# Hash attention and two MLPs on one core: the second head's first hashes one pass later, and the first weights of the next layer converted in consecutive passes

## The chip, the core and the metric

One core of a Trainium2 chip runs the whole program in one launch. The metric is device time in microseconds (us); lower is better. TensorE (PE in the rows) multiplies, VectorE (DVE) and ScalarE (ACT) work element by element, GpSimd (POOL) does some element work on the side, and SyncE (SP) issues the transfers, one after the other in its own order. Each engine works through its own list of instructions in order and waits for the others by semaphores.

## What is computed

Attention in which a query sees only the keys of its own hash bucket, then two MLPs on the result:

```
q_bits = (q @ proj > 0);  k_bits = (k @ proj > 0)          # 6 bits each
mask   = bucket(q_bits) == bucket(k_bits)
attn   = softmax(where(mask, q @ k.T / sqrt(64), -1e9))     # 2 x 8 heads, 768 x 768
x      = attn @ v                                           # 1536 tokens x 512
x      = (silu(x @ w_gate) * (x @ w_val)) @ w_out           # 512 -> 1536 -> 512
h      = x @ w_in;  out = (layernorm(h * softmax(h)) * g_ln) @ w_out2
```

The MLP weights arrive as 64-bit floats. The kernel reads them as pairs of 32-bit words and makes 32-bit floats of them on VectorE.

## The kernel before

**Attention in passes.** The 16 heads are 8 pairs. One pass of the main loop (line 754 and following; its counter is i) takes 128 queries of one head against all 768 keys, so a pair has 12 passes and there are 96. The work is a pipeline over passes. In pass i the loop issues, in this order: `maxima(i)` and `biases(i)` on VectorE (L495, L504); on TensorE `transposes(i - 2)`, which turn the exponentials of pass i - 2 into a two-buffer PSUM tile (L535); hashing and turning work of a later pair; `scores(i + 1)` into a two-buffer PSUM tile (L484); for pass i - 2 the rounding on ScalarE (`highs`, L544) and the rest on VectorE (`lows`, L548), which read the turned exponentials; `values` for an earlier quarter (L570, L574); and `exps(i)` on ScalarE (L520), which read the scores. So the transposes of pass i wait for the `lows` issued in pass i - 1, which free their PSUM buffer, and `scores(i + 1)` wait for `exps(i - 1)`.

**Hashes.** `hashes(p, n)` multiplies the turned heads with the hash weights and VectorE turns signs to bits (L448); four transfers (`move`, L264) then carry the bits of both heads to their places. For the first pair each head has its own `first_hashes(j)`: eight matrix products (L355) into the PSUM tiles `pp` and `av`, which have one buffer each, and then the bits. For the second head (j = 1) the generator is started at line 773; its second step, the bits (L364) and two moves, follows in pass 2.

**First weights.** `early()` (line 713) prepares the first block of `w_gate` and of `w_val`. For each it issues a transfer of 512 KB into one buffer `raw` (L717) and then six VectorE instructions (`to_float32`: L47, L51, L53, L57, L62, L64, in this order). It is a generator: every `go(first_weights)` does one step, and a step is either the transfer or one instruction. The `w_gate` transfer is issued ahead of the loop. So the steps in the loop are six instructions, the `w_val` transfer, and six instructions. Since there is one buffer, the second transfer waits for the last instruction on the first block. The results `w1f` are first used behind the attention (L844).

**What sets the order.** The order on every engine is that in which the code is written (`manual_schedule`). SP's list too: a transfer is issued only when all transfers written ahead of it have been issued, each after its own wait.

Of the kernel before, what the change touches and what calls it, by code (L numbers as in the profile page):

```python
# [28 lines left out]
def run(steps):  # L29
    for _ in steps:  # L30
        pass
# [36 lines left out]
def hash_attention_then_two_mlps(  # L68
# [137 lines left out]
    with at:  # L206
# [13 lines left out]
        SLOTS = 2 * C  # L220
# [3 lines left out]
        def load(p, nm):  # L224

            if p >= len(pairs):
                return
            b, hp = pairs[p]
            t = nat.tile([P, 2, C, D], F32, tag=nm, name=nm)
            src = {"q": q, "k": k, "v": v}[nm]  # L230
            nc.sync.dma_start(
                t, src[b, 2 * hp:2 * hp + 2].rearrange("h (p c) d -> p h c d", c=C)
            )
            raw[p, nm] = t
# [230 lines left out]
        def quarter(h):  # L465


            p, l = divmod(h, 4)
            return (p, l // 2, l % 2) if p == 0 else (p, l % 2, l // 2)
# [5 lines left out]
        def scores(i):  # L475
            if not 0 <= i < NSLOT:
                return
            p, j, n = quarter(i // CH)
            x, c = turned[p, j], n * CH + i % CH
            s = ps_s.tile([P, 2, 512], F32, tag="s", name="s")  # L480
            rows = slice(c * P, (c + 1) * P)
            for a, m, first in ((x["qa"], x["ka"], True), (x["qb"][:MB], x["kb"][:MB], False)):
                for n in range(2):
                    nc.tensor.matmul(  # L484
                        s[:, n, :HALF], a[:, rows], m[:, n * HALF:(n + 1) * HALF],
                        start=first, stop=not first,
                    )
            s_of[i] = s

        def maxima(i):  # L490
            if not 0 <= i < NSLOT:
                return

            top = tops[i % len(tops)]
            nc.vector.tensor_reduce(  # L495
                top[:, 1:2], s_of[i][:, :, :HALF], AX.XY, ALU.max, negate=True
            )

        def biases(i):
            if not 0 <= i < NSLOT:  # L500
                return
            top = tops[i % len(tops)]
            nm = sm.tile([P, 2], F32, tag="nm", name="nm", bufs=3)
            biased = nc.vector.scalar_tensor_tensor(  # L504
                nm, top[:, 1:2].to_broadcast([P, 2]), LONE, top, ALU.is_lt, ALU.mult
            )
            if i > 2:
                bias_of[:] = [biased]
            nm_of[i] = nm
# [16 lines left out]
        def transposes(i, g):  # L526
            if not 0 <= i < NSLOT:
                return
            h, c = divmod(i, CH)
            if c == 0 and g == 0:  # L530
                eh_of[h] = et.tile([P, C, HALF], R32, tag="eh", name="eh")
                el_of[h] = et.tile([P, C, HALF], R32, tag="el", name="el")
            t = ps_t.tile([P, CH, P], F32, tag="t", name="t")
            for m in range(CH):
                nc.tensor.transpose(t[:, m, :], e_of[i][:, g, m * P:(m + 1) * P], idf)  # L535
            t_of[i, g] = t
# [5 lines left out]
        def highs(i, g):  # L542
            if 0 <= i < NSLOT:
                nc.scalar.copy(half_tile(eh_of, i, g), t_of[i, g])  # L544

        def lows(i, g):
            if 0 <= i < NSLOT:
                last_of[i] = nc.vector.tensor_sub(  # L548
                    half_tile(el_of, i, g), t_of.pop((i, g)),
                    half_tile(eh_of, i, g).bitcast(F32),  # L550
                )
# [108 lines left out]
        def go(work):  # L660

            next(work, None)
# [3 lines left out]
        def turning(p, l):  # L666

            if p == 1:

                at = {  # L670
                    0: lambda: turn(p + 1, 0, 2),
                    1: lambda: turn(p + 1, 1, 0),
                    2: lambda: turn(p + 1, 1, 1),
                    3: lambda: turn(p + 1, 1, 2),
                    6: lambda: hashes(p + 1, 0, False),
                    7: lambda: hashes(p + 1, 1, False),
                }
            else:
                if l in (4, 6):
                    hashing[:] = [hashes(p + 1, l // 6)]  # L680
                at = {
                    0: lambda: turn(p + 1, 1, 0),
                    1: lambda: turn(p + 1, 1, 1),
                    3: lambda: turn(p + 1, 1, 2),
                }
                at.update({n: lambda: hashing[0] for n in range(4, 8)})
            at.update({
                9: lambda: turn(p + 2, 0, 0),
                10: lambda: turn(p + 2, 0, 1),
                11: lambda: turn(p + 2, 0, 2),  # L690
            })
            return at[l]() if l in at else iter(())

        def beginning(i):

            at = {
                3: lambda: (turn(1, 0, 0), turn(1, 0, 1, 1)),
                4: lambda: (turn(1, 0, 2), turn(1, 1, 0, 1)),
                5: lambda: (turn(1, 1, 1),),
                6: lambda: (turn(1, 1, 2),),  # L700
                8: lambda: (hashes(1, 0, False),),
                9: lambda: (hashes(1, 1, False),),
                10: lambda: (turn(2, 0, 0),),
                11: lambda: (turn(2, 0, 1),),
            }
            works = at[i]() if i in at else ()
            for work in works:
                go(work)
            yield
            for work in works:  # L710
                go(work)

        def early():

            for n, w in enumerate((w_gate, w_val)):
                t = wp.tile([P, DM], I64, name="raw")
                nc.sync.dma_start(  # L717
                    t.rearrange("p (k f) -> p k f", k=KD),
                    w[:, 0:P].rearrange("(k p) f -> p k f", p=P),
                )  # L720
                yield
                yield from to_float32(nc, t, w1f[n])
                yield
# [22 lines left out]
        with tc.manual_schedule():  # L746
            for p, nm in ((1, "k"), (1, "q"), (0, "v")):
                load(p, nm)
            first_weights = early()
            go(first_weights)  # L750
            hashed = start()
            done = leaving = iter(())
            splits = {}
            for i in range(NSLOT + 9):
                p, l = divmod(i, SLOTS)
                h, part = divmod(i - 5, CH)
                if i < SLOTS:
                    work = beginning(i)
                else:
                    work = turning(p, l)  # L760
                if part == 0:
                    leaving, done = done, results(h - 1)
                    go(done)
                maxima(i)
                if part == 0 and h - 1 >= NQ - 2:
                    go(done)
                biases(i)
                transposes(i - 2, 0)
                if i == 0:
                    go(hashed)  # L770
                transposes(i - 2, 1)
                go(work)
                if i == 1:
                    hashed = first_hashes(1)
                    go(hashed)
                scores(i + 1)
                for g in range(2):
                    highs(i - 2, g)
                    lows(i - 2, g)
                if part == 0:  # L780
                    go(leaving)
                values(h, part)
                if part == 2 and h == NQ - 1:
                    spread(*quarter(h)[::2])
                go(work)
                if i == 2:
                    go(hashed)
                exps(i)
                if i == 0:
                    for of, nm in ((1, "k"), (1, "q"), (0, "v")):  # L790
                        run(split(of, nm))
                splitting(p, l)
                go(done if part == 2 else leaving)
                if part == 2 and h == NQ - 2:
                    widen(*quarter(NQ - 1)[::2], "both")
                if part == 1:
                    go(done)
                    sums(h + 1)
                if l in (3, 9, 11):
                    go(first_weights)  # L800

    AHEAD = 2
# [374 lines left out]
```

## Time and profile before

| | |
|---|---|
| three runs | 699.26, 701.16, 701.88 us; median 701.16 |
| the profiled execution: its time | 700.81 us |
| the profiled execution: its span | 699.0 us |
| busy share of the span | PE 99%, VectorE 80%, ScalarE 49%, GpSimd 21% |
| granted TensorE clock, mean | 0.993 of full speed |

The span runs from the first to the last instruction; the execution's own time is 1.81 us longer. The attention takes about the first 250 us of it; the two MLPs follow. The shares are means over stages. Times in the rows count from the start of the span.

### The profile page before, as it was taken

To read this page: it belongs to the slowest core of one execution; us is meant where nothing else is said; L and a number is where in the kernel's file an instruction comes from. 1 tells how busy PE (TensorE), PEld (TensorE's weight loads), DVE (VectorE), ACT (ScalarE), POOL (GpSimd) and SP (SyncE) were. 2 spreads that over 40 slices of the span, in tenths; PEclk is the share of its full clock that TensorE was granted. 3 is DMA by queue.
4 is the path that set the end of the run, shared out by engine and by line. 5 is a ranking of instruction groups with operands and counts; after the bars stand their busy time and mean duration, and the time that the engine had idled before them with its cause. 6 is when DMAs were issued, how large, how long until landed. Compare 5 with 4: busy or idle time off the path is not lost.

```text
span 699.0 us, 10084 instructions
## 1 busy us (share of the span) xinstructions
PE 690.9 (99%) x3683; PEld 593.2 (85%) x3683; DVE 557.1 (80%) x974; ACT 339.3 (49%) x676; POOL 150.0 (21%) x156
## 2 busy tenths in 40 slices
PE   7999999999999999999999999999999999999997
PEld 4899999999999988888888888888888888888886
DVE  6899999999989998766887877977988886655461
ACT  4888989889898963433123022032133522222222
POOL 7346665556634260000000000000000000000000
PEclk8899999999999999999999999999999999999999
DMA  7654746447161404222223131131321000000001
GB/s 210 163 144 111 185 114 167 118 114 178 38 158 43 133 12 120 91 91 73 109 68 113 60 121 61 60 121 60 112 83 48 1 15 16 31 15 20 27 15 46
DMA packets 36177, 60.59 MB, mean 87 GB/s; under 512 B 4984, under 2 KB 26552, under 8 KB 35616
## 3 DMA queue, kind: packets, MB, share of 16 engines
q1 hardware_dynamic: 36128, 59.95, 29.6%
q8 instruction: 29, 0.48, 0.3%
q14 instruction: 20, 0.16, 0.1%
HBM read 36.71 MB, written 3.15 MB: 57 GB/s over the span
## 4 chain that ended last, share of the span: by engine, by line
PE 95%; issue 2%; DVE 1%; DMA 1%; POOL 1%; SPq 1%; ACT 0%; POOLq 0%; ACTq 0%
PE h L945 28%; PE s L484 10%; PE h L1057 10%; PE t L535 9%; PE av L570 5%; PE y L970 5%; PE y L971 5%; PE y L969 5%; PE av L574 4%; PE o L1108 3%; PE o L1110 3%; PE o L1109 3%; PE pp L443 2%; PE pp L405 2%; PE t L1095 1%
## 5 line engine op out<-in xcount | busy, mean ns | idle before, releaser
L945 PE MATMUL h<-xl,hi 128*128 128x512 f32 x288 | 112.1, 389 | 0.0
L945 PE MATMUL h<-xh,hi 128*128 128x512 f32 x288 | 112.1, 389 | 0.0
L945 PE MATMUL h<-xh,lo 128*128 128x512 f32 x288 | 111.2, 389 | 0.0
L548 DVE TENSOR_TENSOR el<-t,eh 128x384 fp32r<-128x384 f32 x192 | 97.7, 550 | 9.4 <-ACT eh L544 7.1
L520 ACT ACTIVATE e<-s,nm 128x768 f32<-128x768 f32 x96 | 97.9, 1020 | 6.2 <-DVE nm L504 3.0
L1083 POOL TENSOR_TENSOR w<-w,half 128x1 f32<-128x1 f32 x12 | 6.6, 550 | 415.4 <-DVE w L1082 310.2
L544 ACT CAST eh<-t 128x384 fp32r<-128x384 f32 x192 | 84.2, 494 | 21.2 <-PE t L535 19.7
L495 DVE TENSOR_REDUCE top<-s 128x1 f32<-128x768 f32 x96 | 90.6, 943 | 3.0 <-PE s L484 2.8
L535 PE MATMUL t<-idr,e 128*128 128x128 f32 x576 | 81.4, 277 | 0.2 <-DVE el L548 0.2
L535 PEld LDWEIGHTS t<-idr,e 128*128 128x128 f32 x576 | 69.1, 142 | 9.4 <-DVE el L548 3.3
L570 PE MATMUL av<-eh,vs 128*128 128x384 f32 x186 | 64.0, 344 | 0.0
L945 PEld LDWEIGHTS h<-xh,hi 128*128 128x128 f32 x288 | 54.1, 188 | 11.3
L945 PEld LDWEIGHTS h<-xl,hi 128*128 128x128 f32 x288 | 54.1, 188 | 11.1
L945 PEld LDWEIGHTS h<-xh,lo 128*128 128x128 f32 x288 | 54.0, 188 | 11.1
L955 ACT CAST ah<-sg 128x512 fp32r<-128x512 f32 x36 | 22.4, 622 | 74.9 <-DVE sg L953 74.9
L484 PE MATMUL s<-ka,qa 128*128 128x384 f32 x192 | 56.7, 377 | 0.1
L970 PE MATMUL y<-al,hi 128*128 128x512 f32 x144 | 56.0, 389 | 0.0
L971 PE MATMUL y<-ah,lo 128*128 128x512 f32 x144 | 56.0, 389 | 0.0
L969 PE MATMUL y<-ah,hi 128*128 128x512 f32 x144 | 56.0, 389 | 0.0
L953 DVE TENSOR_TENSOR sg<-h,sg 128x512 f32<-128x512 f32 x36 | 24.8, 689 | 37.4 <-PE h L945 22.5
L574 PE MATMUL av<-el,vs 128*64 128x384 f32 x155 | 52.3, 338 | 0.0
L916 ACT CAST hi<-wf 128x1024 fp32r<-128x1024 f32 x17 | 17.9, 1051 | 69.8 <-DVE wf L64 69.8
(203 smaller groups left out, 1429.5 us busy)
## 6 DMA issues: line engine op xcount, KB each, us to landing
raw<-in_moe_w_out_dram SPq DMA_DIRECT2D x10, 1024.0 KB
raw<-in_moe_w_gate_dram SPq DMA_DIRECT2D x12, 512.0 KB
raw<-in_moe_w_val_dram SPq DMA_DIRECT2D x12, 512.0 KB
ka<-kt SPq DMA_DIRECT2D x30, 192.0 KB
raw<-in_moe_w_in_dram SPq DMA_DIRECT2D x4, 1024.0 KB
v<-in_v_dram SPq DMA_DIRECT2D x8, 384.0 KB
kb<-kt SPq DMA_DIRECT2D x15, 192.0 KB
qb<-qa SPq DMA_DIRECT2D x15, 192.0 KB
```

The source lines that it names most:

```text
L484: nc.tensor.matmul(s[:, n, :HALF], a[:, rows], m[:, n * HALF:(n + 1) * HALF], start=first, stop=not first,)
L495: nc.vector.tensor_reduce(top[:, 1:2], s_of[i][:, :, :HALF], AX.XY, ALU.max, negate=True)
L520: nc.scalar.activation(e, s_of.pop(i)[:, :, :HALF], AF.Exp, bias=nm[:, 1:2], scale=nm[:, 0:1], accum_out=total_of[p, n][:, j, c:c + 1],)
L535: nc.tensor.transpose(t[:, m, :], e_of[i][:, g, m * P:(m + 1) * P], idf)
L544: nc.scalar.copy(half_tile(eh_of, i, g), t_of[i, g])
L548: last_of[i] = nc.vector.tensor_sub(half_tile(el_of, i, g), t_of.pop((i, g)), half_tile(eh_of, i, g).bitcast(F32),)
L570: nc.tensor.matmul(av, vj[:, c], eh_of[h][:, c, :], start=c == 0, stop=c == C - 1)
L574: nc.tensor.matmul(*low, start=False, stop=False)
L945: nc.tensor.matmul(ps[n], a[:, n, kk, :], x[:, kk, blk * BLK:(blk + 1) * BLK], start=kk == 0 and a is hi and x is xh, stop=kk == KD - 1 an ...
L969: nc.tensor.matmul(p, hi[:, cols], ah, start=f == t * FT, stop=False)
L970: nc.tensor.matmul(p, hi[:, cols], al, start=False, stop=False)
L971: nc.tensor.matmul(p, lo[:, cols], ah, start=False, stop=f == (t + 1) * FT - 1)
```

## The change

Two conditions in the main loop change. The first hashes of the second head are issued in pass 2 and no longer in pass 1, between the transposes and the scores of that pass; their bits and moves stay in pass 2. And `first_weights` is stepped in every pass from 3 to 23, no longer in the passes 3, 9 and 11 of each pair (3, 9, 11, 15, 21, 23, 27 and so on). There are 13 steps; before, the last one fell in pass 51, now it falls in pass 15.

```diff
@@ -770,7 +770,7 @@
                     go(hashed)
                 transposes(i - 2, 1)
                 go(work)
-                if i == 1:
+                if i == 2:
                     hashed = first_hashes(1)
                     go(hashed)
                 scores(i + 1)
@@ -796,7 +796,7 @@
                 if part == 1:
                     go(done)
                     sums(h + 1)
-                if l in (3, 9, 11):
+                if 2 < i < 2 * SLOTS:
                     go(first_weights)
```

| step of `early()` | before, in pass | now, in pass |
|---|---|---|
| `w_gate`: L47, L51, L53, L57, L62, L64 | 3, 9, 11, 15, 21, 23 | 3, 4, 5, 6, 7, 8 |
| `w_val`: transfer (L717) | 27 | 9 |
| `w_val`: L47, L51, L53, L57, L62, L64 | 33, 35, 39, 45, 47, 51 | 10, 11, 12, 13, 14, 15 |

On TensorE, at the first passes of the loop (`s` are scores, `t` turned exponentials, `pp` and `av` the hash tiles), the difference reads:

```order
 L484 MATMUL s<-ka,qa 128x384 x2
 L484 MATMUL s<-kb,qb 128x384 x2
+L484 MATMUL s<-ka,qa 128x384 x2
+L484 MATMUL s<-kb,qb 128x384 x2
+L535 MATMUL t<-idr,e 128x128 x6
 L355 MATMUL pp<-kt,hash_k 128x512
 L355 MATMUL av<-kt,hash_k 128x256
```

The scores of pass 2 and the first six transposes now stand ahead of the eight hash products, not behind them.

On SP, around pass 9, the list before reads as follows (`bits` are the hash bits of the second pair, `q` a load of a later pair):

```order
L264 DMA qb<-bits 12x768
L264 DMA kb<-bits 12x768
L264 DMA qb<-bits 12x768
L264 DMA kb<-bits 12x768
L231 DMA q<-in_q_dram 128x2x384
L638 DMA low<-xf 64x384
```

And now:

```order
L264 DMA qb<-bits 12x768
L264 DMA kb<-bits 12x768
L264 DMA qb<-bits 12x768
L264 DMA kb<-bits 12x768
L717 DMA raw<-in_moe_w_val_dram 128x4x128
L231 DMA q<-in_q_dram 128x2x384
L638 DMA low<-xf 64x384
```

The `w_val` transfer has come to stand right behind the four moves of pass 9; before, it stood 34 rows further down.

On VectorE, from the bits of pass 9 to the maxima of pass 11, the list before is:

```order
L448 TENSOR_SCALAR bits<-pp,over,weigh 128x384
L583 TENSOR_SCALAR total<-total 128x6
L584 RECIPROCAL r<-total 128x6
L51 TENSOR_SCALAR w1f_105<-w1f_105 128x512
L495 TENSOR_REDUCE top_160<-s 128x1
L504 SCALAR_TENSOR_TENSOR nm<-top_160 128x2
L548 TENSOR_TENSOR el<-t,eh 128x3x128 x2
L495 TENSOR_REDUCE top_161<-s 128x1
```

And now (`raw` is the buffer of the transfer, `w1f_106` the result for `w_val`):

```order
L448 TENSOR_SCALAR bits<-pp,over,weigh 128x384
L583 TENSOR_SCALAR total<-total 128x6
L584 RECIPROCAL r<-total 128x6
L495 TENSOR_REDUCE top_160<-s 128x1
L504 SCALAR_TENSOR_TENSOR nm<-top_160 128x2
L548 TENSOR_TENSOR el<-t,eh 128x3x128 x2
L47 TENSOR_SCALAR w1f_106<-raw 128x512
L495 TENSOR_REDUCE top_161<-s 128x1
```

L51 has left pass 9, and pass 10 ends with the first instruction that reads the newly transferred `raw`.

## Rows read from the trace of the kernel before

**Rows 1.** The profile page: busy time, share of the span and instructions of each engine.

```profile
PE 690.9 (99%) x3683; PEld 593.2 (85%) x3683; DVE 557.1 (80%) x974; ACT 339.3 (49%) x676; POOL 150.0 (21%) x156
```

**Rows 2.** Timeline of PE: transposes opening passes 39, 51, 63, 75 (start, duration).

```profile
112.99 0.82 PE L535 MATMUL t<-idr,e 128*128 128x128 f32 x6
...
142.94 0.81 PE L535 MATMUL t<-idr,e 128*128 128x128 f32 x6
...
172.60 0.82 PE L535 MATMUL t<-idr,e 128*128 128x128 f32 x6
...
202.30 0.82 PE L535 MATMUL t<-idr,e 128*128 128x128 f32 x6
```

**Rows 3.** Timeline of PE: transposes opening passes 10, 11 and 12.

```profile
41.00 0.82 PE L535 MATMUL t<-idr,e 128*128 128x128 f32 x6
...
43.41 0.82 PE L535 MATMUL t<-idr,e 128*128 128x128 f32 x6
...
45.84 0.81 PE L535 MATMUL t<-idr,e 128*128 128x128 f32 x6
```

**Rows 4.** Timeline of VectorE, pass 9's bits to pass 12; idle time before in brackets.

```profile
39.87 0.67 DVE L448 TENSOR_SCALAR bits<-pp,over,weigh 128x384 fp32r<-128x384 f32 x1
...
41.06 0.95 DVE L495 TENSOR_REDUCE top<-s 128x1 f32<-128x768 f32 x1
...
42.12 1.01 DVE L548 TENSOR_TENSOR el<-t,eh 128x384 fp32r<-128x384 f32 x2
43.05 0.95 DVE L495 TENSOR_REDUCE top<-s 128x1 f32<-128x768 f32 x1
...
44.64 1.02 DVE L548 TENSOR_TENSOR el<-t,eh 128x384 fp32r<-128x384 f32 x2 [0.45 <-ACT eh L544]
...
46.39 0.94 DVE L495 TENSOR_REDUCE top<-s 128x1 f32<-128x768 f32 x1
```

**Rows 5.** Timeline of PE and ScalarE at the second head's first hashes.

```profile
14.81 0.50 PE L355 MATMUL pp<-kt,hash_k 128*128 128x512 f32 x1 [1.52 <-DVE qb L379]
...
15.17 0.19 ACT L520 ACTIVATION_READ_ACCUMULATOR e<-s,nm 128x1 f32 x1
...
17.84 1.01 PE L484 MATMUL s<-ka,qa 128*128 128x384 f32 x2
```

**Rows 6.** What touches `w1f` and `raw`: ns least/median/most, first and last start.

```profile
L47 DVE TENSOR_SCALAR w1f<-raw x2: 415/416/416, 25.2 to 100.7; 128x512 int32<-128x512 int32 x2
L51 DVE TENSOR_SCALAR w1f<-w1f x2: 383/611/839, 40.8 to 105.6; 128x512 f32<-128x512 f32 x2
L53 DVE TENSOR_SCALAR w1f<-w1f x2: 416/654/892, 45.6 to 115.3; 128x512 int32<-128x512 int32 x2
L57 DVE SCALAR_TENSOR_TENSOR w1f<-raw,w1f x2: 681/682/682, 55.1 to 130.4; 128x512 int32<-128x512 int32 x2
L64 DVE CUSTOM_DVE_ANT_0 w1f<-raw,w1f x2: 683/875/1067, 75.6 to 145.2; 128x1024 uint16<-128x1024 uint16 x2
...
L62 DVE TENSOR_SCALAR raw<-raw x2: 418/763/1108, 70.7 to 135.3; 128x512 int32<-128x512 uint32 x2
```

**Rows 7.** Waits between 24 and 46 us: us in total, times, longest.

```profile
DVE el L548 <- ACT eh L544: 1.5, 4, 0.4
```

**Rows 8.** Timeline of GpSimd beside the first L53.

```profile
44.34 1.84 POOL L246 TENSOR_TENSOR vs<-v,vs 128x768 fp32r<-128x768 f32 x1 [0.59 <-DVE nm L504]
```

**Rows 9.** Timeline of SP (start, issue time): pass 9's first move, the next load, `w_val`.

```profile
40.56 0.80 SPq L264 DMA_DIRECT2D qb<-bits  x1
...
43.87 0.46 SPq L231 DMA_DIRECT2D q<-in_q_dram  x1
...
85.75 0.54 SPq L717 DMA_DIRECT2D raw<-in_moe_w_val_dram  x1
```

**Rows 10.** Windows: length, busy by engine, granted clock, transfer share, GB/s.

```profile
16.30:23.10 6.80, 6.80 (x25) 5.73 (x25) 4.68 (x7) 3.40 (x7) 4.43 (x3) 0.50 0.41 120
87.20:89.20 2.00, 2.00 (x16) 1.89 (x15) 1.71 (x4) 1.58 (x4) 1.47 (x2) 1.00 0.82 265
```

## The prediction, made before the changed kernel was run

> **What bounds the kernel now.** The page gives TensorE 99% of the span [rows 1], but its busy time is modelled, and VectorE is nearly as full in the attention, so I tested which of the two sets the pace. First over a whole pair of heads. From pass 39 to 51 VectorE runs three of the conversion instructions (passes 39, 45, 47), and the transposes that open those passes on PE stand 142.94 - 112.99 = 29.95 us apart; from pass 63 to 75 it runs none, and they stand 202.30 - 172.60 = 29.70 apart [rows 2]. Three VectorE instructions in or out are worth 0.25 us. Then pass by pass: passes 10 and 11 take 43.05 - 41.06 = 1.99 and 46.39 - 43.05 = 3.34 us on VectorE [rows 4], but 2.41 and 2.43 on PE [rows 3]. PE goes at its own pace and VectorE follows unevenly behind. So the time changes by what PE loses: idle time, and time at the lower clock.
>
> VectorE is not far from being waited for. The transposes of pass 11 need the PSUM buffer that the first `lows` of pass 10 frees. The two `lows` are one row, 42.12 with 1.01 us [rows 4], so the first ends near 42.63; PE takes the buffer at 43.41 [rows 3]: 0.78 us of slack. For pass 12 it is 44.64 + 0.51 = 45.15 against 45.84: 0.69. A VectorE delay above 0.7 us here is a delay of PE.
>
> **The hashes of the second head.** Before, PE sat idle 1.52 us, until 14.81, for the `pp` and `av` tiles, and then ran the eight products until 17.84 [rows 5]. Now the scores of pass 2 stand in that place, and they need the scores buffer that the first exponentials free: 15.17 + 0.19 = 15.36. That is 0.55 us more idle time on PE; the products cost the same later. The bits now come right behind the products in the same pass, but the second head's scores begin only with pass 5's `scores(6)`, so they hide there. Part of the 0.55 is taken back where passes 5 to 9 wait for ScalarE anyway [rows 7]. I take +0.3 on VectorE's clock by pass 9; ends 0 and +0.6.
>
> **More conversions in passes 4 to 8.** Pass 3 keeps its L47. Added are L51 0.38, L53 0.42, L57 0.68, L62 0.42 and L64 0.68 (the least of each, [rows 6]): 2.58 us. Each hides about 0.08 in the hand-over to the next instruction, as 42.12 + 1.01 overlaps 43.05 by 0.08 [rows 4]: -0.40. VectorE's waits for ScalarE's casts between 24 and 46 us are 1.5 in four [rows 7], of which 0.45 belongs to pass 11 [rows 4]; the other 1.05 gives cover. That leaves 2.58 - 0.40 - 1.05 = 1.13, with the hashes 1.4. Against it, the same instruction can take longer: L53 took 0.42 once and 0.89 once [rows 6], the latter at 45.58 while a GpSimd instruction ran from 44.34 to 46.18 [rows 8]. One or two such meetings in passes 6 to 8, where GpSimd splits the next heads, add up to 0.9; I take 0.4. So the bits of pass 9, which end at 39.87 + 0.67 = 40.54 before, end 1.8 us later; ends 1.0 and 2.6. (PE is then about 1.1 late, by the slack above.)
>
> The Trainium skill (SBUF — State Buffer, section "SBUF: two separate sides") says that VectorE and GpSimd share a pair of ports under an exclusive lock, so that the loser blocks for the whole instruction. The trace agrees in kind, L53 being held 0.47 us here; by the rule a meeting could cost up to the 1.84 of the GpSimd row, and two such would make the 0.4 a 3.7 and the sum 710.9.
>
> **The transfer in pass 9: the main term.** SP issues the four bit moves from 40.56 and gets to the next row, the `q` load, at 43.87 [rows 9]: 3.33 us after the bits. In the change the `w_val` transfer takes that place. How long does it take to land? Before, it was issued at 85.75 [rows 9], and the window from 87.2 to 89.2 moved 2.0 us x 265 GB/s = 530 KB [rows 10], its 512 KB. So it landed 3.4 us after its issue. Bounds: 0.5 of issue and 2.0 of moving, with nothing ahead of it: 2.5; one microsecond more than seen, for moves and loads ahead: 4.4. In before's clock it lands at 40.54 + 3.33 + 3.4 = 47.3, and 1.8 later by the paragraph above: 49.1.
>
> VectorE reaches L47 at the end of pass 10. Before, that pass ended at 43.13; L51's 0.30 has left pass 9, and the delay is 1.8: 44.6. So VectorE waits about 4.5 us for the transfer, with pass 11's maxima queued behind it. L47 itself adds 0.42 - 0.08, so those start at 49.4. From maxima to the first `lows` freed is 42.12 - 41.06 + 0.51 = 1.57 [rows 4]. PE starts the transposes of pass 12 at 51.0, against 45.84 before [rows 3]: **+5.2 us of PE time**, some 4 of it idle in one piece, since PE has nothing else to do in order, and ScalarE waits with it. The queue is in order on both sides: nothing behind L47 on VectorE, nothing behind the transposes on PE can go ahead.
>
> **The clock after it.** At the start a 1.52 us gap [rows 5] was followed by 6.8 us at a granted clock of 0.50 [rows 10], which is the lower level, 1.2 GHz in place of 2.4. A gap of 4 us should not do better. If all 6.8 come, PE loses 3.4 us of work; if half of it, 1.7; if none, 0. I take 1.7.
>
> **What is given back.** Out of passes 21 to 51 go eight instructions (passes 21, 23, 33, 35, 39, 45, 47, 51). By VectorE's clock that is 5.6 us (adding their rows), but on PE three were worth 0.25, so eight are 0.7; I take -0.5, ends 0 and -0.7. Added in passes 10 to 15 are, L47 apart, five instructions where there were two; they run while PE is slow, so I take 0. If the clock does not fall they have only the slack as cover: up to +1.0. GpSimd and the other transfers get their work later by the same shift, and nothing waits for `w1f` before the end of the attention.
>
> **Sum.** 5.2 + 1.7 - 0.5 = +6.4 us. The profiled execution took 700.81, so 707.2; the median of the runs is 0.35 above it, 701.16, so **707.6 us**. The case's own range: downward 0.8 (conversions), 0.9 (landing), 1.7 (clock), 0.2; upward 0.8, 1.0, 1.7, 1.0. They will not all fall together; as root of the sum of squares 2.1 and 2.3: 705.5 to 709.9.
>
> **Rivals.**
> 1. *The transfer is hidden; not slower.* Place: SP's list in pass 9. If the block has landed when VectorE comes to L47 plus the slack, at 44.6 + 0.7 = 45.3, PE loses only the 1.1 it was late, less 0.5: +0.6, 701.8. It decides at the issue: it would have to go out by 45.3 - 3.4 = 41.9. For it: the transfer is small and the engines are not full. Against: the four moves before it wait for the bits at 42.3, so 41.9 lies ahead of them all.
> 2. *VectorE is the bound after all.* Then all that leaves it counts. Of the ten instructions taken from their passes (9, 11 and the eight), L51 is 0.38, L53 0.89, the eight 5.6: 6.9, less 10 x 0.08, 6.1. Added are passes 4 to 8 with 1.13 + 0.4, L51 in 11 and L53, L57 and L62 in 12 to 14 (0.38 + 0.42 + 0.68 + 0.42 - 0.32 = 1.6), and the wait with L47, 4.8: 7.9. Net +1.8 and the hashes' 0.3: 703.3. Against: [rows 2, 3].
> 3. *The clock does the opposite at the start.* If the 6.8 slow microseconds [rows 10] do not come, because scores and products now run on in one piece behind the gap, PE gains up to 3.4: 707.6 - 3.4 = 704.2. Against: the gap grows from 1.52 to 2.07.
> 4. *Worse.* The slow stretch lasts its 6.8 us, 1.7 more, or two conversions meet a whole GpSimd instruction of 1.84 us [rows 8] each, 3.7 - 0.4 = 3.3 more: 709.3 to 710.9. For it: GpSimd has such instructions in passes 6 to 9. Against: L53 was held for 0.47 only [rows 6].
>
> A result below 697.7 needs rivals 1 and 3 together: 701.8 - 3.4 = 698.4 is still not enough without more.
>
> **Chances.** Forecast 0.72, rival 1 0.10, rival 2 0.06, rival 3 0.04, rival 4 0.08. What this kernel's measurement can tell from no change is about 0.5%, 3.5 us: slower means above 704.7, faster below 697.7. The forecast's case lies above 704.7 but for a tenth of it: 0.65 and rival 4's 0.08 make 0.73 slower, with a little of rival 3 0.74; 0.03 faster, the rest 0.23. The 8-in-10 range reaches down to take in rival 2 and 3 and up to rival 4's middle: 702.8 to 710.3; rival 1 and the tail stay out.
>
> **What would show it.** Right: L717 issued near 45.7, right behind the four moves; a VectorE wait of 3.5 to 5.5 us on the transfer in front of L47; PE idle about 4 us in front of the transposes of pass 12, which start near 51; a granted clock of 0.5 for 3 us or more thereafter; from pass 16 on PE at the intervals of before, 29.7 a pair. Wrong: no such wait (rival 1); intervals on PE that shrink in passes 33 to 51 by more than 0.5 in sum (rival 2); a clock above 0.5 between 16 and 23 (rival 3). If passes 4 to 9 come 3 us late, the conversions were mis-sized.

## The result and the profile after

Three runs of the changed kernel took 707.67, 707.78 and 709.0 us; the median is 707.78 against 701.16 before, a ratio of 1.0105 with a 95% interval of 1.007 to 1.0141. The profiled execution took 707.78 us with a span of 705.9, so the spans of the two profiled executions differ by 6.9 us. Forecast were 707.6 us and slower. The total is right, but as shown below several of its terms were off in opposite directions.

The page of the changed kernel: the busy times, and the shares of the chain that ended last.

```profile
PE 692.3 (98%) x3683; PEld 593.0 (84%) x3683; DVE 557.7 (79%) x974; ACT 339.7 (48%) x676; POOL 148.9 (21%) x156
...
PE 91%; DVE 4%; issue 2%; DMA 1%; ACT 0%; SPq 0%; POOL 0%; POOLq 0%; ACTq 0%
```

The page hardly differs from [rows 1], as counts of instructions are the same. The chain tells more: VectorE has 4% of it, where it had 1% before, so the end now hangs on VectorE in more places. Where they lie shows on PE. Here are the transposes that open passes 4, 11, 12, 13, 14, 18 and 24 (start, duration, idle time before in brackets; each opens with six transposes, and a smaller count comes from the edge of the stretch that was read).

```profile
23.21 1.01 PE L535 MATMUL t<-idr,e 128*128 128x128 f32 x6 [0.33 <-DVE el L548]
...
43.20 1.01 PE L535 MATMUL t<-idr,e 128*128 128x128 f32 x6 [0.15 <-DVE el L548]
...
50.31 1.54 PE L535 MATMUL t<-idr,e 128*128 128x128 f32 x6 [4.33 <-DVE el L548]
...
54.80 1.03 PE L535 MATMUL t<-idr,e 128*128 128x128 f32 x6
...
57.44 0.81 PE L535 MATMUL t<-idr,e 128*128 128x128 f32 x6
...
67.46 0.71 PE L535 MATMUL t<-idr,e 128*128 128x128 f32 x5
...
83.29 0.81 PE L535 MATMUL t<-idr,e 128*128 128x128 f32 x6
```

Pass 12 answers to the last of [rows 3] (45.84): PE sat idle for 4.33 us in front of it. Cutting both spans at the same passes says where the 6.9 us are (before: pass 4 at 24.90, 11 at 43.41, 12 at 45.84, 18 at 59.96):

| stretch | before | after | difference |
|---|---|---|---|
| start to pass 4 | 24.90 | 23.21 | -1.69 |
| pass 4 to 11 | 18.51 | 19.99 | +1.48 |
| pass 11 to 12 | 2.43 | 7.11 | +4.68 |
| pass 12 to 18 | 14.12 | 17.15 | +3.03 |
| pass 18 to the end | 639.04 | 638.44 | -0.60 |

Everything that costs lies between passes 4 and 18. VectorE's timeline from pass 6 shows it, with conversions at L57, L62, L47 and L51.

```profile
30.53 1.30 DVE L57 SCALAR_TENSOR_TENSOR w1f<-raw,w1f 128x512 int32<-128x512 int32 x1
...
33.74 1.41 DVE L62 TENSOR_SCALAR raw<-raw 128x512 int32<-128x512 uint32 x1
...
40.27 0.67 DVE L448 TENSOR_SCALAR bits<-pp,over,weigh 128x384 fp32r<-128x384 f32 x1
...
42.60 1.01 DVE L548 TENSOR_TENSOR el<-t,eh 128x384 fp32r<-128x384 f32 x2
48.30 0.43 DVE L47 TENSOR_SCALAR w1f<-raw 128x512 int32<-128x512 int32 x1 [4.69 <-DMA raw<-in_moe_w_val_dram]
48.64 0.95 DVE L495 TENSOR_REDUCE top<-s 128x1 f32<-128x768 f32 x1
...
50.64 1.40 DVE L51 TENSOR_SCALAR w1f<-w1f 128x512 f32<-128x512 f32 x1
```

L47 waits 4.69 us for the transfer, and the maxima of pass 11 (L495) are queued behind it. In [rows 4] they stood at 43.05 without a wait. The rest of what the rows say is in the durations: L57 took 1.30 us, L62 1.41 and L51 1.40, against 0.68, 0.42 and 0.38 as the least in [rows 6]. SP's list has the cause of the wait (start, issue time).

```profile
40.96 0.80 SPq L264 DMA_DIRECT2D qb<-bits  x1
...
43.44 0.71 SPq L264 DMA_DIRECT2D kb<-bits  x1
44.21 0.52 SPq L717 DMA_DIRECT2D raw<-in_moe_w_val_dram  x1
```

The bits end at 40.27 + 0.67 = 40.94, four moves go out behind them, and L717 is issued 3.27 us after the bits. The transfer has landed when L47 starts, 4.1 us after its issue. GpSimd's timeline has the cause of the long durations.

```profile
29.81 1.47 POOL L242 TENSOR_TENSOR ks<-k,one 128x768 fp32r<-128x768 f32 x1 [8.90 <-PE pp L405]
33.03 1.83 POOL L246 TENSOR_TENSOR ks<-k,ks 128x768 fp32r<-128x768 f32 x1 [1.75 <-DVE nm L504]
...
49.93 1.81 POOL L246 TENSOR_TENSOR vs<-v,vs 128x768 fp32r<-128x768 f32 x1 [5.71 <-DMA qb<-kt]
```

Each of the three long conversions begins while one of these runs, and ends 0.55, 0.29 and 0.30 us after it: L57 at 31.83 against 31.28, L62 at 35.15 against 34.86, L51 at 52.04 against 51.74. So a conversion that meets a GpSimd instruction does most of its work when that is over.

The windows give the granted clock (length, busy by engine, clock, transfer share, GB/s), as [rows 10] did.

```profile
7.40:14.30 6.90, 6.90 (x26) 4.97 (x26) 3.64 (x5) 3.23 (x8) 6.67 (x7) 0.51 0.89 283
14.30:44.00 29.70, 27.22 (x174) 22.50 (x173) 28.70 (x52) 22.82 (x51) 14.29 (x9) 1.00 0.55 144
...
48.40:55.20 6.80, 4.89 (x20) 4.60 (x21) 6.70 (x14) 3.69 (x7) 1.81 (x1) 0.50 0.67 163
```

The clock was at the lower level for 6.8 us, from near the end of PE's idle stretch on. In the last row PE is busy for 4.89 us, which is all the time from the opening of pass 12 at 50.31 to 55.20, and VectorE for 6.70 of the 6.80 us. So both are full there, and the columns do not say which of them sets the pace. Pass 12 takes 54.80 - 50.31 = 4.49 us on PE, against 2.41 before. At the start the lower level stands in another place than in [rows 10].

### The profile page after: what moved, and what is told of

Its sections match the earlier page's. It is cut to its first block, busy times and chain, and to the rows that moved or that the text cites. A ratio compares the mean times of both kernels' runs of the same rounds, so it can differ in the third digit from the quotient of the medians.

```text
span 705.9 us, 10082 instructions
## 1 busy us (share of the span) xinstructions
PE 692.3 (98%) x3683; PEld 593.0 (84%) x3683; DVE 557.7 (79%) x974; ACT 339.7 (48%) x676; POOL 148.9 (21%) x156
## 4 chain that ended last, share of the span: by engine, by line
PE 91%; DVE 4%; issue 2%; DMA 1%; ACT 0%; SPq 0%; POOL 0%; POOLq 0%; ACTq 0%
PE h L945 28%; PE h L1057 9%; PE s L484 9%; PE t L535 8%; PE y L970 5%; PE y L969 5%; PE y L971 5%; PE av L570 4%; PE av L574 4%; PE o L1108 3%; PE o L1110 3%; PE o L1109 3%; PE pp L443 2%; DVE top L495 2%; PE pp L405 1%
## 5 line engine op out<-in xcount | busy, mean ns | idle before, releaser
L495 DVE TENSOR_REDUCE top<-s 128x1 f32<-128x768 f32 x96 | 90.6, 944 | 1.0 <-PE s L484 0.8
```

The source lines that it names most:

```text
L495: nc.vector.tensor_reduce(top[:, 1:2], s_of[i][:, :, :HALF], AX.XY, ALU.max, negate=True)
```

## The experiments

No kernel leaves work out; two add products that nobody reads. The ratios are against runs of the kernel before on the same chip, whose median was 701.53 us for the first four kernels, 701.03 for the next four and 701.34 for the last three. Each diff is against the changed kernel. The theory was that the wait for the transfer, made by its place on SP's list, is the main cost. Its rivals were that the conversions on VectorE cost as such, that the lower clock does, or that the hashes do.

**Each half alone.** First the hashes without the conversions:

```diff
-                if 2 < i < 2 * SLOTS:
+                if l in (3, 9, 11):
                     go(first_weights)
```

> Only the first hashes of the second head are moved to pass 2; the conversions stay in passes 3, 9 and 11 of each pair. Theory A (the loss is all the conversions', the hash move is worth the +0.3 us of the prediction): 701 to 702 us, no change that can be measured. Rival B (the profiled execution of the changed kernel reached pass 3 at 21.5 us and not at 23.2, and that gain belongs to the move): 699 to 700 us. If the gain is only the place in which the slow clock happened to fall in that execution, the time stays at 701 and the granted clock of the first 25 us explains the start of pass 3.

It took 700.22 us, between the two expected ranges, a ratio of 0.9987 [0.9978, 0.9997]: the move costs nothing, and gains 0.2 to 1.5 us. The place on VectorE in the kernel before, the maxima of pass 2:

```profile
19.53 0.96 DVE L495 TENSOR_REDUCE top<-s 128x1 f32<-128x768 f32 x1 [2.02 <-PE s L484]
```

and the same with the hashes moved, first on VectorE, then on PE the scores and the products of the hashes:

```profile
17.45 0.94 DVE L495 TENSOR_REDUCE top<-s 128x1 f32<-128x768 f32 x1
```

```profile
15.44 1.01 PE L484 MATMUL s<-ka,qa 128*128 128x384 f32 x2 [1.84 <-ACT e L520]
...
18.02 0.77 PE L355 MATMUL pp<-kt,hash_k 128*128 128x512 f32 x1
```

PE's idle time does grow, from 1.52 us [rows 5] to 1.84. But scores now come first, so VectorE's wait of 2.02 us is gone. Pass 4 opens at 23.55 in place of 24.90. Now the conversions without the hashes:

```diff
-                if i == 2:
+                if i == 1:
                     hashed = first_hashes(1)
```

> Only the conversions are moved to passes 3 to 15; the first hashes of the second head stay in pass 1. Theory A (the whole loss comes from the conversions, through the wait for the transfer): 707 to 708 us, with a VectorE wait of 4 to 5 us in front of L47 and PE idle for about 4 us in front of pass 12. Rival B (the hash move saves 1.7 us in the changed kernel): 709 to 710 us.

It took 709.8 us, 1.0109 [1.0092, 1.0126], by the ratios as much as the whole change (1.0105). The time itself is the rival's: in the profiled executions pass 4 opens at 24.85, as before and 1.64 us later than in the changed kernel. L47 waits 4.79 us. The loss is that of the conversions.

**The transfer ahead of the moves.** The step that issues it is written before the bits and moves of pass 9.

```diff
+                if i == 9:
+                    go(first_weights)
                 go(work)
...
-                if 2 < i < 2 * SLOTS:
+                if 2 < i < 2 * SLOTS and i != 9:
```

> The changed kernel, but in pass 9 the step that issues the w_val transfer is written ahead of the four moves of the hash bits; all conversions stay in the same passes. Theory A (the place of the transfer behind the moves on SP is what makes VectorE wait): the transfer goes out about 5 us earlier, the wait in front of L47 is under 0.5 us, PE has no gap and the clock stays up: 701.5 to 703.5 us. Rival B (conversions in consecutive passes cost the time by themselves, through VectorE): 705 us or more, without the wait.

704.94 us, 1.0041 [1.0025, 1.0056]. SP, VectorE and PE (passes 11 and 12) of this kernel:

```profile
41.27 0.37 SPq L717 DMA_DIRECT2D raw<-in_moe_w_val_dram  x1
...
43.85 0.80 SPq L264 DMA_DIRECT2D qb<-bits  x1
```

```profile
46.42 0.98 DVE L47 TENSOR_SCALAR w1f<-raw 128x512 int32<-128x512 int32 x1
```

```profile
46.09 1.01 PE L535 MATMUL t<-idr,e 128*128 128x128 f32 x6 [0.16 <-DVE el L548]
...
48.98 1.01 PE L535 MATMUL t<-idr,e 128*128 128x128 f32 x6
```

The issue now lies ahead of the first move, L47 has no wait (it takes 0.98 us, as it meets a GpSimd instruction), and passes 11 to 12 take 2.89 us in place of 7.11. The place on SP's list makes the wait. The clock does not fall after the start either. And yet passes 12 to 18 take 16.68 us against 14.12: something other than wait and clock costs 2.5 us there, and the time is 1.4 us above what was expected of theory A.

**Is it the clock?** Eighteen unread products keep PE at work in the gap before pass 12; everything else stays.

```diff
+                if i == 2 * C:
+                    t = ps_p.tile([P, 512], F32, tag="pp", name="pp")
+                    for _ in range(18):
+                        nc.tensor.matmul(
+                            t, idr, turned[1, 1]["kt"][:, :512], start=True, stop=True
+                        )
```

> The changed kernel, with 18 products of 512 columns that nobody reads put on PE in front of the transposes of pass 12; at about 0.22 us each they fill 3.9 of the 4.3 us in which PE stood idle, and lengthen nothing that PE has to wait for anyway. Theory A (the slow clock after the gap costs about 2.5 us on top of the wait): the granted clock stays 1.0 behind 45 us, passes 12 and 13 take 2.4 us each on PE, and the time is 705 to 706 us. Rival B (VectorE sets the pace of those passes, the clock costs nothing): 707.5 to 708 us with the clock up.

The median was 710.34, 1.0111 [1.009, 1.0132], above what either side expected. The profiled execution, 706.0 us, is the fastest of six that went up to 711.39. PE of that execution, passes 12 and 18, and a window behind the gap:

```profile
44.34 4.38 PE L771 MATMUL pp<-kt,idr 128*128 128x512 f32 x18
48.90 1.01 PE L535 MATMUL t<-idr,e 128*128 128x128 f32 x6 [0.18 <-DVE el L548]
...
65.59 0.82 PE L535 MATMUL t<-idr,e 128*128 128x128 f32 x6
```

```profile
50.00:54.00 4.00, 3.46 (x25) 2.90 (x24) 3.93 (x9) 3.13 (x7) 0.35 (x1) 1.00 0.53 136
```

The recorded clock stays at 1.00, and the durations bear it out: the transposes of pass 12 take 1.01 us, against 1.54 in the changed kernel. But passes 12 to 18 still take 65.59 - 48.90 = 16.69 us. So with the clock up 16.69 - 14.12 = 2.57 us of the 3.03 are still lost, and only 17.15 - 16.69 = 0.46 go with the lower clock. VectorE is full in the window (3.93 of 4.00), PE is not (3.46). Then the same two kernels without the conversions behind the gap: the steps stop with L47 in pass 10 and go on from pass 27.

```diff
-                if 2 < i < 2 * SLOTS:
+                if 2 < i < 11 or i > 2 * SLOTS and l in (3, 9, 10):
```

> The changed kernel up to L47 in pass 10, with its wait for the transfer and the gap on PE; the five conversions behind it come only from pass 27 on. In the changed kernel passes 12 to 18 took 17.15 us on PE against 14.12 before, in the filled gap 16.69 with the clock up. Theory A (there VectorE with its conversions set the pace and hid the slow clock; without them the clock shows): 6.8 us at a granted 0.5 behind the gap, passes 12 to 18 on PE 16 to 17 us, 2 to 2.5 us of that being the clock's. Rival B (the slow clock costs next to nothing even so): 14.1 to 14.6 us. Time 704 to 707 us by A, 703 to 705 by B.

> As gap_pause, with 18 unread products of 512 columns on PE in the gap in front of pass 12. Theory A: the clock stays at 1.0 and passes 12 to 18 take 14.1 to 14.6 us on PE, 2 us or more less than in gap_pause. Rival B: the same as gap_pause within 0.4 us.

709.21 us, 1.012 [1.0103, 1.0136], and with the products 707.3, 1.0092 [1.0072, 1.0112]. Passes 12 and 18 without the products, and with them:

```profile
53.36 0.93 PE L535 MATMUL t<-idr,e 128*128 128x128 f32 x4 [4.43 <-DVE el L548]
...
69.22 0.82 PE L535 MATMUL t<-idr,e 128*128 128x128 f32 x6
```

```profile
50.51 1.01 PE L535 MATMUL t<-idr,e 128*128 128x128 f32 x6 [0.21 <-DVE el L548]
...
64.82 0.82 PE L535 MATMUL t<-idr,e 128*128 128x128 f32 x6
```

15.86 us without the products (clock 0.51 from 53.8 to 57.3) and 14.31 with them (clock 1.00, transposes back at 1.01 us), 14.12 before. So four kernels answer for passes 12 to 18:

| | clock up | lower clock |
|---|---|---|
| no conversions in passes 11 to 15 | 14.31 | 15.86 |
| with them | 16.69 | 17.15 |

The lower clock costs 1.55 us where VectorE has nothing extra to do and 0.46 where it has the conversions. Read the other way, the conversions cost 2.38 us with the clock up and 1.29 with it down. About 1.1 us of each hides behind the other, so the 3.03 us can't be divided between them in only one way. Without the conversions the lower clock thus does what theory A said, at 15.86 a little less than its 16 to 17. The numbers come from one profiled execution each, and PE worked at the lower level for 3.5 us without the conversions and 4.89 with them, so in the changed kernel the clock by itself may cost more than 1.55. The medians don't show these differences: the kernel without conversions and products was expected at 704 to 707 us and took 709.21, more than the changed kernel. Its pass 4 opens at 26.22 in the profiled execution, 3.0 us later than in the changed kernel; the section on the prediction comes back to the start.

**Conversions later, or spread.** All from pass 27 on in passes 3, 9 and 10 of a pair, with the hashes as changed; and one step in every second pass from 3 to 27:

```diff
-                if 2 < i < 2 * SLOTS:
+                if l in (3, 9, 10) and i > 2 * SLOTS:
```

```diff
-                if 2 < i < 2 * SLOTS:
+                if 2 < i < 28 and i % 2:
```

> The hashes in pass 2 as in the changed kernel; all conversion steps from pass 27 on, three per pair (passes 3, 9 and 10 of each), the transfer six passes ahead of its first reader. Theory A (from pass 16 on PE sets the pace and conversions are free; the first passes are where VectorE has no room): 699 to 700.5 us, below the kernel before by 1 to 2 us, no wait on the transfer. Rival B (conversions cost the same wherever they stand): 700.2 us, the time of the hash move alone, or more.

> The hashes in pass 2; one conversion step in every second pass from 3 to 27, so as many in the first two pairs as the changed kernel has but two, spread out, and the transfer two passes ahead of its first reader with no bit moves in front of it on SP. Theory A (what costs beside the wait is that consecutive passes leave VectorE no pass to catch up in): 700 to 701.5 us. Rival B (conversions in the first two pairs cost whatever their spacing): 703 to 705 us.

The first took 700.64 us, 1.0001 [0.9988, 1.0014], the second 705.41, 1.0053 [1.0035, 1.0072]. Where the conversions come late, the time lies where the ranges of the two theories meet and does not tell them apart, but the pairs from pass 24 to 72 with three of them in each take 29.69 to 29.91 us, against 29.70 without any: they cost 0.2 us a pair. In every second pass the time is the rival's or a little more, and passes 4 to 36 take 84.90 us on PE, against 80.85 before. So room alone does not help: there L53 took 1.19, L62 1.36 and 1.23, and L57 1.36 us, each begun while a GpSimd instruction ran and ended 0.27 to 0.55 after it. L47 waited 0.90 us there although the transfer was issued two passes ahead of it; it landed 64.03 - 58.58 = 5.45 us after its issue.

**A pass or two between transfer and L47.** No step in pass 10, or none in passes 10 and 11:

```diff
-                if 2 < i < 2 * SLOTS:
+                if 2 < i < 2 * SLOTS and i != 10:
```

```diff
-                if 2 < i < 2 * SLOTS:
+                if 2 < i < 2 * SLOTS and i not in (10, 11):
```

> The changed kernel, with no step in pass 10: L47 comes in pass 11, one pass (about 2.6 us) later, and waits about 4.7 - 2.6 = 2.1 us. By the slack of some 0.5 us on PE the pass that holds the wait should be 1.5 to 2.5 us longer on PE. Open is the clock: by theory A a gap of 1.5 to 2 us is enough for the granted 0.5 (at the start 1.5 us was); by rival B it is not, and the clock stays up. Time 705 to 707.5 us.

> The changed kernel, with no conversion step in passes 10 and 11: the transfer stays behind the four moves in pass 9, L47 comes in pass 12. Theory A (the wait is a matter of the distance between issue and first reader): no wait or under 0.3 us at L47, the gap on PE gone, the clock up behind 26 us, 704 to 706 us, as with the transfer ahead of the moves. Rival B (something else in passes 9 to 12 costs the 4.7 us): 707 us or more.

709.57 us, 1.0114 [1.0098, 1.0131], and 705.99, 1.0068 [1.0055, 1.008]. L47 with one pass between, then with two:

```profile
52.28 0.43 DVE L47 TENSOR_SCALAR w1f<-raw 128x512 int32<-128x512 int32 x1 [3.34 <-DMA raw<-in_moe_w_val_dram]
```

```profile
51.70 0.43 DVE L47 TENSOR_SCALAR w1f<-raw 128x512 int32<-128x512 int32 x1 [0.18 <-DMA raw<-in_moe_w_val_dram]
```

One pass takes 1.4 us from the wait, less than the 2.6 expected, and the time is above the expected range; two take it away, and 4.65 us over before remain by the medians: once more a loss with hardly any wait. With one pass between, PE was idle for 2.27 us, and the clock was 0.50 from 55.8 to 59.1.

**Out of GpSimd's way.** In the code each of GpSimd's splitting instructions (L242, L246) waits for the newest `biases` (`behind`, called in `split`). The rows agree: in the changed kernel all six between 29 and 50 us begin 0.08 to 0.14 us after a `biases` has ended, also where the row names another releaser. A conversion written behind `lows` begins soon after that: in the three rows above 0.7 us after GpSimd's instruction. So here each conversion stands between maxima and biases, ahead of the release (passes 4 to 9 and, with the transfer ahead of the moves, 11 to 16).

```diff
                 maxima(i)
...
+                if 3 < i < 2 * SLOTS and i != 10:
+                    go(first_weights)
                 biases(i)
...
+                if i == 9:
+                    go(first_weights)
                 go(work)
...
-                if 2 < i < 2 * SLOTS:
-                    go(first_weights)
```

> As ahead_of_moves (no wait for the transfer), but each conversion stands right behind the maxima of a pass and ahead of its biases; the twelve instructions fall in passes 4 to 9 and 11 to 16. GpSimd's long instructions are issued behind the biases of a pass, so at this place none should be running. Theory A (of what is left without the wait, most is conversions held by GpSimd: L57, L62, L51 and L62 took 1.30, 1.41, 1.40 and 1.03 us for 0.68, 0.42, 0.38 and 0.42 of work, 3.2 us in all): each takes its least time, and passes 4 to 18 take 2 to 3 us less on PE than in ahead_of_moves (39.5): 36.5 to 37.5; time 702 to 703 us. Rival B (being held matters little, or later biases cost as much as is saved): 39 us or more, 704.5 to 706 us.

700.79 us, 0.9991 [0.9979, 1.0004]. What touches `w1f` and `raw` in the attention (ns least/median/most), and PE at passes 4 and 18:

```profile
L51 DVE TENSOR_SCALAR w1f<-w1f x2: 416/417/418, 27.0 to 45.7; 128x512 f32<-128x512 f32 x2
...
L57 DVE SCALAR_TENSOR_TENSOR w1f<-raw,w1f x2: 675/678/681, 32.0 to 50.4; 128x512 int32<-128x512 int32 x2
...
L62 DVE TENSOR_SCALAR raw<-raw x2: 419/490/560, 34.5 to 52.9; 128x512 int32<-128x512 uint32 x2
```

```profile
23.57 1.01 PE L535 MATMUL t<-idr,e 128*128 128x128 f32 x6
...
59.15 0.82 PE L535 MATMUL t<-idr,e 128*128 128x128 f32 x6
```

All are back near their least times; only the first L62 still met the end of a GpSimd instruction (0.56 us). Passes 4 to 18 take 59.15 - 23.57 = 35.58 us, against 39.50 with the transfer ahead but the conversions behind `lows`, and 35.06 before (59.96 - 24.90). The gain is larger than theory A expected (36.5 to 37.5). So 3.9 us of the cost belong to the place of the conversions within the pass. Being held accounts for nearly all of it: with the transfer ahead of the moves L57, L62, L47, L51 and L62 lost 0.62 + 0.99 + 0.56 + 1.02 + 0.61 = 3.80 us, here 0.14. (They also stand one pass later. For the second block a pass or two more took none of this loss away, as the runs above show; for the first it was not tried.) Twelve conversions between passes 4 and 18, where before had three, then cost 0.5 us on the path, and nothing that the times can tell. This version is 1% faster than the changed kernel; that it beats the kernel before is not shown, as its interval reaches over 1.

## Why the prediction came out right in sum

| step of the prediction | taken | measured |
|---|---|---|
| opening of pass 12: hashes, conversions, wait | +5.2 | +4.47 (50.31 - 45.84) |
| the lower clock behind the gap, by itself | +1.7 | +1.55 (15.86 - 14.31) |
| conversions in passes 11 to 15, on top of it | 0 | +1.29 (17.15 - 15.86) |
| what is left in passes 12 to 18 without either | 0 | +0.19 (14.31 - 14.12) |
| given back from pass 18 on | -0.5 | -0.60 |
| sum | +6.4 | +6.9 |

**What bounds the kernel: right, but not in passes 12 to 17.** PE sets the pace in the pairs from pass 24 on, where VectorE has at most three conversions in a pair. From pass 24 to 72 the changed kernel takes 29.66 to 29.70 us a pair, like the pairs without conversions in [rows 2], and eight instructions taken out give back 0.60 us. Rival 2, by which each of their 5.6 us counts, is ruled out for these passes. In passes 12 to 17, with a conversion in almost every pass, PE waits for VectorE once the clock is up: in the filled kernel in front of passes 13, 16 and 17 (0.54, 0.17 and 0.25 us).

**The transfer: right, place and size.** L717 came 3.27 us behind the bits (3.33 taken), the wait was 4.69 (4.5) and PE's idle stretch 4.33 (4). The landing took 4.1 us after the issue, where 3.4 was taken with bounds of 2.5 and 4.4; in the kernel without the hash move and in the filled one it took 3.9, with a step in every second pass 5.45. Rival 1 asked for an issue by 41.9: it came at 44.21. With the issue at 41.27 there was no wait.

**The hashes: the sign was wrong.** The step "+0.3" counted PE's idle time, which grows as it says, and left out that VectorE's wait of 2.02 us for the scores goes. Alone the move gives 0.9 us. In the profiled execution 1.69 us are gained up to pass 4, with the lower clock for 6.9 us (7.4 to 14.3) where before it had two stretches of 3.4 and 6.9 (9.5 to 12.9, 16.3 to 23.2). That is rival 3's mechanism in part, and its sign, a clock above 0.5 between 16 and 23, did show. But the move does not cause it reliably: among the kernels that have the move, pass 4 opened at 23.2 to 23.6 with 6.9 to 10.2 us of the lower clock at the start, and at 26.0 to 26.2 with 13 to 17. The two kernels with products have no lower clock on record there (23.13 and 21.55), but durations show some. In the one without the conversions the same product takes

```profile
8.09 0.79 PE L355 MATMUL pp<-qa,hash_q 128*128 128x512 f32 x1
...
17.86 0.50 PE L355 MATMUL pp<-qa,hash_q 128*128 128x512 f32 x1
```

and PE's instructions from 6.2 to 13.7 us are longer in like measure. So a recorded 1.00 alone does not show that the clock was up, and durations have to be looked at beside it.

**Meetings with GpSimd: mis-sized.** The step took "one or two such meetings ... I take 0.4". L57 and L62 alone lost 0.62 + 0.99 = 1.61 us in passes 6 and 7, so that the bits of pass 9 ended 17.73 us after pass 4's opening (40.94 - 23.21) against 15.64 before (40.54 - 24.90), 2.1 later, not 1.5. Over both blocks these instructions lost 3.2. The row of the one L53, held for 0.47 us, was too mild a sample. Rival 4 had asked for two such meetings of a whole GpSimd instruction; there were four, each for a part of one. The Trainium skill (SBUF — State Buffer, section "SBUF: two separate sides") has VectorE and GpSimd exclude each other for a whole instruction on the ports that they share; the trace agrees, as the three conversions ended only 0.29 to 0.55 us after the GpSimd instruction that they met.

**The clock and the conversions behind the gap: the clock's term held, the 0 did not.** The clock fell as said, for 6.8 us, and by itself it costs 1.55 us (1.7 taken), measured where PE worked at the lower level for 3.5 us and not 4.89. "They run while PE is slow, so I take 0" is half true: of the 2.38 us that the conversions cost with the clock up, 1.09 hide behind the slow PE and 1.29 do not. The text had their cost at "up to +1.0" if the clock stays up. It missed that GpSimd holds them here too: L51 in pass 11 (1.40 us) and L62 in pass 14 (1.03 us) lost 1.02 + 0.61 = 1.63 us.

**How much of it is luck.** In passes 12 to 18 the sum was 1.33 us too low, in front of pass 12 it was 0.73 too high, and the latter is itself a balance: 1.69 us gained at the start, where 0.3 of loss was taken, against more than was taken between passes 4 and 12. That these nearly cancel, and that 707.6 stands so close to 707.78, is luck; that the wait for the transfer is the main term is not.

**What stays open.** Why the lower clock at the start falls where it does in each execution. It matters, as the profiled executions of the kernels with the hash move open pass 4 some 3 us apart, the later ones with more of it, and their times differ likewise: the six executions with the transfer ahead of the moves took 703.0 to 703.9 or 706.0 to 706.3 us, and the profiled one, with pass 4 at 26.16, is of the second kind. So medians of a few executions carry this difference, and the intervals inside a profile do not. It may also be why four of the six executions of the kernel with the products and all conversions were 4.0 to 5.4 us slower than the one whose rows are known, which opened pass 4 at 21.55, the earliest of all; without rows of the others that is not shown, and the mean clock of 1.0 that two of the four have does not exclude it, by what was said above of a recorded 1.00. What is concluded from that kernel rests on the intervals inside the one profile, not on its median.

## What to carry to other kernels

Before work is put into the gaps of a full engine, look at what shares an order with it: a transfer stands behind every transfer written ahead of it on its queue, and an instruction that waits for it stops all that is queued behind. Where VectorE and GpSimd work side by side, put VectorE's extra instructions ahead of the one that releases GpSimd, not behind it; here that was worth 3.9 us with the same instructions. Two costs in one stretch, as a lower clock of one engine and extra work on another, can hide behind each other: take out each alone and both together, and compare intervals of the same stretch before dividing a loss between them.

## What the runs showed of the hardware

A conversion on VectorE that reads one tensor of 128 x 512 was held as much as one that reads two: L62 took 1.41 us in place of 0.42, L51 1.40 in place of 0.38, while GpSimd instructions of 1.81 and 1.83 us ran; L57, which reads two, took 1.30 in place of 0.68 beside one of 1.47. An idle stretch of PE of 2.27 us was followed by the lower level of the clock for 3.3 us; one of 4.33 by 6.8, one of 4.43 by 3.5. The transfer of 512 KB landed 3.9 to 5.45 us after its issue where VectorE waited for it. For 7.5 us at the start of an execution whose recorded clock was 1.00 throughout, the durations of PE's products were those of the lower level (0.79 against 0.50 us for the same product).
